# Projections as column tiles in two halves, a tail split by tile, and SyncE's general path in front: one change to a two-part attention kernel

## The chip, the cores and the metric

One core of a Trainium2 chip. The metric is the device time of one launch in microseconds (us): the median of a kernel's runs in the fast state. A granted TensorE clock, as a share of full speed, comes with each run. A profiled run also has a span, from its first to its last instruction, which is 1.7 to 1.9 us shorter than that run's own time.

## The reference

Two independent halves, joined along the last axis; inputs and outputs are bfloat16.

```python
def reference(A_x, A_wq, A_wk, A_wv, A_wo, B_x, B_wqkv, B_w_phi, B_wo):
    # A: softmax attention, S=2048, D=512, 32 query heads of 16, one key/value head
    q = (x @ wq).reshape(B, S, 32, 16).transpose(0, 2, 1, 3);  k = x @ wk;  v = x @ wv
    p = softmax(einsum("bhqd,bkd->bhqk", q, k) * 16 ** -0.5)
    a = einsum("bhqk,bkd->bhqd", p, v)...reshape(B, S, 512) @ wo
    # B: linear attention; features [softmax(u), softmax(-u)] of u = q @ w_phi and u = k @ w_phi
    kv = einsum("bhsf,bhsd->bhfd", phi_k, v);  z = phi_k summed over s
    o = einsum("bhqf,bhfd->bhqd", phi_q, kv) / (einsum("bhqf,bhf->bhq", phi_q, z) + 1e-6)
    b = o...reshape(B, S, 512) @ wo
    return concatenate([a, b], axis=-1)
```

## The kernel before

A small planner inside the kernel makes the program when it is built. Every piece of work is a job with an engine and an assumed duration; the planner simulates the engines, picks what to issue next, and writes one fixed, in-order program for each engine. The chip gets these orders as they stand. So a constant of the planner changes the order, and with it how many score blocks go which way.

Scores of part A are made in quads of four blocks. A quad goes one of two ways: ScalarE exponentiates it (two instructions `f_PT<-f_ps`, 128x1024), or VectorE turns it into bit patterns of powers (four `f_Z<-f_ps`) which GpSimd shifts (`f_Z<-f_Z`). Either way TensorE multiplies with the values in groups of four column tiles. All projections are done between these groups.

```python
    def job(self, name, eng, dur, fn, after=(), mode=None, nb=0, frees=(), rel=0.0, prio=5.0, ok=None):
        j = _Job(name, eng, dur, fn, after, mode, nb, frees, rel, prio, ok)
        ...
    # one of 92 projections: four full 128x128 matmuls in one go
    job(("pq", ch), "pe", 0.86, ..., mode="full", nb=1, ...)
    def proj_q(self, ch):
        ...
            for dc in range(4):
                mm = pe.matmul(ps[:, bank, :], lhsT=self.wq[:, dc, A * 128:A * 128 + 128],
                               rhs=xT[:, dc, qc * 512:(qc + 1) * 512], start=(dc == 0), stop=(dc == 3))
    # normalisation of a finished pair of heads: a VectorE product of two SBUF tensors
    job(("on", sc), "dve", 0.60, ...finish_sc3...)
    # jobs that the planner never lets run beside a GpSimd shift:
    LOCK = ("dS", "qw")
    # the planner's choice between a locked VectorE job and a shift that asked first
    if j.eng == "dve" and j.name[0] in self.LOCK:
        s, j = next((p for p in picks if p[1].eng == "pool" and p[1].asked <= s + self.NEAR ...), (s, j))
    # end of each engine's program: the fast path jumps over the general path
                e.br_eq(r, 0, there + "_over", there).branch_hint(ahead)
                with e.bass.body(there, valid_engines=[e.engine]):
                    ...general(name, e)...
    # tail: output tiles 2 and 3 copied and sent by ScalarE, 0 and 1 by VectorE and SyncE
        for i in (2, 0, 3, 1): ...
```

## Time and profile before

| | before |
|---|---|
| time, median of 3 runs | 713.73 us (712.76 to 714.05) |
| span of the profiled run | 711.0 us |
| double exponentials of part A on ScalarE | 700 |
| bit conversions on VectorE | 648 |
| first exponential starts | 9.25 us |
| last exponential ends | 695.18 us |

One budget is used all through, because ScalarE leads:

span = first exponential + floor + stalls + tail.

The floor is 0.904 us (the median from start to start) for each double exponential and 0.477 for each of the 64 exponentials of part B. The stalls are what is left up to the end of the last exponential. The tail is the rest. The stalls can also be summed from the trace, as everything above 0.905 us from start to start of neighbouring double exponentials; this sum is called the excess.

One more line: the normalisation. In this trace the three with no shift of GpSimd beside them took 681 to 691 ns and the slowest with one 1375, so the mean time hints at how much GpSimd slowed them.

```profile
L1879 DVE TENSOR_TENSOR f_On<-f_accS,f_denS 128x512 bf16<-128x512 f32 x16 | 15.3, 958 | 0.8 <-DMA f_denS<-f_denS 0.8
```

A line of the page has: line of the kernel, engine, operation, out<-in, shapes, count | busy us, mean ns of one | idle us of the engine just before, and what ended most of it.

### The profile page before, as it was taken

The page shows a single profiled execution, that of the slowest core. Times are in us where ns is not written, and L with a number is a line of the kernel's source. Part 1 is how long each engine was busy: PE and PEld are TensorE (multiplying, and loading weights), DVE is VectorE, ACT ScalarE, POOL GpSimd, SP SyncE. Part 2 cuts the span into 40 slices and gives each one's busy share as a digit, 9 for nine tenths or more (in the row PEclk, how much of TensorE's full clock was granted, in tenths as well). Part 3 has the DMA queues.
Part 4 walks back from the last instruction along what each step waited for, and adds up shares of the span by engine and source line. Part 5 has one row for each costly group of instructions (what it writes and reads, how often), then busy time and mean ns, then how long its engine had stood idle before and what let it go on. Part 6 is the DMA issues. An engine that isn't in the chain of part 4 may idle for free.

```text
span 711.0 us, 18172 instructions
## 1 busy us (share of the span) xinstructions
PE 669.8 (94%) x7493; PEld 211.0 (30%) x7548; DVE 620.6 (87%) x1039; ACT 683.7 (96%) x771; POOL 521.8 (73%) x522
## 2 busy tenths in 40 slices
PE   8999999999999999999999999999999999999995
PEld 3222223222323223332222322323332323333322
DVE  4789899998999999999788987889878989989974
ACT  5999999999999999999999999999999999999992
POOL 4488877777778667876878777678878787787870
PEclk9999999999999999999999999999999999999998
DMA  6611233110112110111110111111111210111212
GB/s 136 134 16 29 41 38 80 8 10 7 9 13 38 11 12 5 12 9 13 9 8 15 17 19 17 16 16 23 21 16 10 27 24 20 17 14 16 32 16 53
DMA packets 47890, 18.28 MB, mean 26 GB/s; under 512 B 38708, under 2 KB 45940, under 8 KB 47800
## 3 DMA queue, kind: packets, MB, share of 16 engines
q1 hardware_dynamic: 45400, 16.23, 18.0%
q8 instruction: 60, 0.98, 0.6%
q10 hardware_dynamic: 2400, 0.82, 0.5%
q14 instruction: 30, 0.25, 0.1%
HBM read 2.28 MB, written 4.19 MB: 9 GB/s over the span
## 4 chain that ended last, share of the span: by engine, by line
ACT 47%; PE 30%; DVE 20%; issue 1%; DMA 1%; POOL 1%; ACTq 0%; DVEq 0%
ACT f_PT L1647 45%; DVE f_Z L1752 11%; PE f_ps L1592 10%; PE f_ps L1812 8%; PE f_ps L1694 4%; PE f_ps L2246 2%; DVE f_ssum L2070 1%; DVE f_vS L2104 1%; ACT f_ET L2161 1%; PE f_ps L1582 1%; PE f_ps L1898 1%; DVE f_Wk L2216 1%; DMA f_AxT<-in_A_x_dram 1%; PE f_ps L2056 1%; DVE f_On L1879 1%
## 5 line engine op out<-in xcount | busy, mean ns | idle before, releaser
L1647 ACT ACTIVATE f_PT<-f_ps 128x1024 bf16<-128x1024 f32 x700 | 654.5, 1093 | 12.4 <-PE f_ps L1592 9.8
L1782 POOL INT64_ADD f_Z<-f_Z x486 | 512.7, 1055 | 167.5 <-DVE f_Z L1752 128.1
L1752 DVE TENSOR_SCALAR f_Z<-f_ps 128x512 int16<-128x512 f32 x648 | 426.0, 683 | 52.7 <-PE f_ps L1592 50.1
L1592 PE MATMUL f_ps<-f_QA,f_KR 32*128 32x512 bf16 x2048 | 280.2, 385 | 14.9 <-ACT f_PT L1647 11.3
L1812 PE MATMUL f_ps<-f_Z,f_VK 128*32 128x512 f16 x2592 | 227.5, 386 | 4.2 <-DVE f_Z L1752 1.6
L1592 PEld LDWEIGHTS f_ps<-f_QA,f_KR 32*128 32x128 bf16 x2048 | 70.4, 91 | 254.4 <-ACT f_PT L1647 224.8
L1694 PE MATMUL f_ps<-f_PT,f_VA 128*32 128x512 bf16 x1400 | 131.6, 385 | 0.1
L1812 PEld LDWEIGHTS f_ps<-f_Z,f_VK 128*32 128x32 bf16 x2592 | 56.4, 94 | 105.4 <-issue 61.2
L1694 PEld LDWEIGHTS f_ps<-f_PT,f_VA 128*32 128x32 bf16 x1400 | 33.6, 94 | 47.8 <-issue 44.7
L2216 DVE TENSOR_TENSOR f_Wk<-f_ps,f_wq 128x512 bf16<-128x512 f32 x32 | 21.9, 683 | 3.6 <-PE f_ps L2205 3.6
L1413 PE MATMUL f_ps<-f_ones,f_zero 128*128 128x512 bf16 (+4 forms) x112 | 20.2, 364 | 1.3 <-POOL f_zero L1432 1.3
L1419 DVE COPY f_accS<-f_ps 128x512 f32<-128x512 f32 x31 | 21.1, 680 | 0.0
L2104 DVE TENSOR_TENSOR f_vS<-f_ps,f_rs 128x1024 bf16<-128x1024 f32 x16 | 19.7, 1229 | 0.2 <-PE f_ps L2094 0.2
L2070 DVE TENSOR_REDUCE f_ssum<-f_Ek 128x64 f32<-128x1024 bf16 x16 | 19.3, 1205 | 0.0
L2161 ACT ACTIVATE f_ET<-f_ps 128x512 bf16<-128x512 f32 x32 | 18.8, 689 | 0.1
L2064 ACT ACTIVATE f_Ek<-f_ps 128x512 bf16<-128x512 f32 x32 | 18.2, 655 | 0.0
L1419 DVE CAST f_outB<-f_ps 128x512 bf16<-128x512 f32 x16 | 10.9, 683 | 6.7 <-PE f_ps L2246 6.7
L2154 PE MATMUL f_ps<-f_BxT,f_Wq 128*128 128x512 bf16 x56 | 14.8, 381 | 1.9 <-issue 1.0
L2246 PE MATMUL f_ps<-f_Bwo,f_oT 128*128 128x512 bf16 x57 | 15.0, 381 | 1.5 <-issue 1.0
L2094 PE MATMUL f_ps<-f_Bwv,f_BxT 128*128 128x512 bf16 x56 | 15.0, 381 | 1.2 <-DVE f_Z L1752 0.8
L1879 DVE TENSOR_TENSOR f_On<-f_accS,f_denS 128x512 bf16<-128x512 f32 x16 | 15.3, 958 | 0.8 <-DMA f_denS<-f_denS 0.8
L2056 PE MATMUL f_ps<-f_Wk,f_BxT 128*128 128x512 bf16 x53 | 14.1, 380 | 1.8 <-issue 1.5
(95 smaller groups left out, 281.7 us busy)
## 6 DMA issues: line engine op xcount, KB each, us to landing
f_denS<-f_denS SPq DMA_DIRECT2D x124, 30.0 KB, 3.1
out_dram<-f_outB SPq DMA_DIRECT2D x16, 128.0 KB, 1.8
f_denC<-f_accS SPq DMA_DIRECT2D x124, 2.0 KB, 1.7
f_denS<-f_denC SPq DMA_DIRECT2D x124, 2.0 KB, 1.7
out_dram<-f_outA SPq DMA_DIRECT2D x14, 128.0 KB, 2.8
f_On<-f_Ot SPq DMA_DIRECT2D x60, 16.0 KB, 1.8
f_Bwv<-in_B_wqkv_dram SPq DMA_DIRECT2D x1, 512.0 KB, 4.2
f_Bwo<-in_B_wo_dram SPq DMA_DIRECT2D x1, 512.0 KB, 4.5
```

The source lines that it names most:

```text
L1419: self.add("dve", lambda v: v.tensor_copy(out=out, in_=in_), reads=reads, writes=writes)
L1592: return pe.matmul(self.ps[:, bank, :], lhsT=self.KR[32 * g:32 * g + 32, sc % 2, kap * 128:(kap + 1) * 128], rhs=self.QA[32 * g:32 * g + 3 ...
L1647: self.add("act", lambda a: a.activation(out=PT[:, sl[0]:sl[0] + size, :], in_=ps[:, b0:b0 + size, :], func=ACT.Exp), reads=[("PS", b0 + i ...
L1694: mm = pe.matmul(ps[32 * g:32 * g + 32, bank, :], lhsT=VA[:, kap, :], rhs=PT[:, slots[g], :], start=start, stop=stop, tile_position=(0, 32 ...
L1752: self.add("dve", lambda v: v.tensor_scalar(out=o, in0=ps[:, bank, :], scalar1=self.Z1, scalar2=self.Z0, op0=ALU.mult, op1=ALU.add), reads ...
L1782: fn = lambda g: g.int64_add(out=b, in0=a, in1=256 * t * 0x1000100010001)
L1812: mm = pe.matmul(ps[32 * g:32 * g + 32, bank, :], lhsT=self.VK[:, t, kap, :], rhs=Zf[:, sl[g], :], start=start, stop=stop, tile_position=( ...
L2070: self.add("dve", lambda v: v.tensor_reduce(out=ssum[:, r, :], in_=Ek[:, r].rearrange("p a h f -> p (a h) f"), axis=AX.X, op=ALU.add), rea ...
L2104: self.add("dve", lambda v: v.tensor_tensor(out=vS[:, :, :, 0:16], in0=v3, in1=rs.unsqueeze(3).to_broadcast([128, 2, 32, 16]), op=ALU.mult ...
L2161: self.add("act", lambda e: e.activation(out=self.ET[:, sl, :], in_=self.ps[:, bank, :], func=ACT.Exp, scale=1.0 - 2.0 * a), reads=[("PS", ...
L2216: self.add("dve", lambda v: v.tensor_tensor(out=o, in0=i, in1=w.unsqueeze(3).to_broadcast([128, 2, 16, 16]), op=ALU.mult), reads=[("PS", b ...
L2246: mm = pe.matmul(ps[:, bank, :], lhsT=oT[:, r, C, :], rhs=self.Bwo[:, C, :], start=(C == 0), stop=(C == 3))
```

## The change

Its intent: a whole projection delays the next scores, so do it in the value products' own tiling mode and in two halves between them; shorten the tail; take a jump off the end; start a little earlier. A dozen constants of the planner were changed with it, and normalisations were locked. The core of the diff:

```diff
     def job(self, name, eng, dur, fn, after=(), mode=None, nb=0, ...):
+        if nb and name[0] in self.SPLIT and dur > 0.8:
+            first = (name[0] + "0",) + name[1:]
+            self.job(first, eng, dur / 2, self.of_part(fn, 0), after, mode, nb, (), rel, prio, ok)
+            return self.job(name, eng, dur / 2, self.of_part(fn, 1), [first], mode, 0, frees, 0.0, self.SECOND)
...
+    def terms(self):
+        return range(4) if self.part_no is None else range(2 * self.part_no, 2 * self.part_no + 2)
...
-            for dc in range(4):
-                mm = pe.matmul(ps[:, bank, :], lhsT=self.wq[:, dc, A * 128:A * 128 + 128], rhs=xT[...], start=(dc == 0), stop=(dc == 3))
+            for dc in terms:
+                for g in range(4):
+                    mm = pe.matmul(ps[32 * g:32 * g + 32, bank, a:a + n], lhsT=self.wq[:, dc, A * 128 + 32 * g:A * 128 + 32 * g + 32], rhs=xT[...], start=(dc == 0), stop=(dc == 3), tile_position=(0, 32 * g))
... (the same in five other projections)
-        for i in (2, 0, 3, 1):
-            o, eng = oa[:, i, :], "act" if i > 1 else "dve"
+        for i in range(4):
+            o = oa[:, i, :]
+            if i % 2 == 0:   # ScalarE copies tiles 0 and 2, VectorE adds up tiles 1 and 3
...
-    LOCK = ("dS", "qw")
+    LOCK = ("dS", "qw", "on", "kvfin")
-    PLEFT = 8.0   QS = 0.9   ZLOW = 4   LEFT = 8   AGE = 3.0   AGED = 0.8   DBUSY = 3.0   T_B = (54.0, 600.0)
+    PLEFT = 20.0  QS = 0.5   ZLOW = 3   LEFT = 16  AGE = 2.0   AGED = 0.6   DBUSY = 5.0   T_B = (43.0, 620.0)
+    SPLIT = ('bk', 'bv', 'bq', 'pq', 'op', 's8')   SECOND = 1.3   FIRST = dict(sp=2)
...
+                if first is not None:                  # SyncE only
+                    S.emit(name, e, sems, k, first)
+                    e.br(there + "_main")              # early jump over the general path
+                    slow()                             # the general path
+                    e.bass.switch_bb(there + "_main", outer)
...
+                    e.br_ne(r, 0, there, there + "_over")   # at the end: fall through
```

(Constants shown several to a line. Cut: the first 128 key columns and the first query chunk done in halves, some small part B reductions, the flag's place.)

## The prediction

> **What bounds the kernel now.** I read the page first: busy shares, the chain, then the costliest groups.
>
> ```profile
> PE 669.8 (94%) x7493; PEld 211.0 (30%) x7548; DVE 620.6 (87%) x1039; ACT 683.7 (96%) x771; POOL 521.8 (73%) x522
> ...
> ACT 47%; PE 30%; DVE 20%; issue 1%; DMA 1%; POOL 1%; ACTq 0%; DVEq 0%
> ...
> L1647 ACT ACTIVATE f_PT<-f_ps 128x1024 bf16<-128x1024 f32 x700 | 654.5, 1093 | 12.4 <-PE f_ps L1592 9.8
> L1752 DVE TENSOR_SCALAR f_Z<-f_ps 128x512 int16<-128x512 f32 x648 | 426.0, 683 | 52.7 <-PE f_ps L1592 50.1
> ```
>
> ScalarE is busy 96%, nearly all of it in 700 double exponentials, and leads the chain. Score blocks come in quads of four; a quad is exponentiated either by ScalarE (two instructions, 700/2 = 350 quads) or as bits by VectorE and GpSimd (four instructions, 648/4 = 162 quads). The planner inside the kernel decides which, so a change may move work between engines.
>
> Second, ScalarE's waits and the chain in order of time, because a busy ScalarE is not one at its best pace:
>
> ```profile
> ACT f_PT L1647 <- PE f_ps L1592: 9.8, 12, 6.1
> ACT f_ET L1946 <- DVE f_ET L1942: 5.9, 1, 5.9
> ```
> ```profile
> 9.27 66.34 ACT f_PT L1647 x72
> ...
> 524.88 33.01 ACT f_PT L1647 x36
> ...
> 694.40 0.98 PE f_ps L1812 x16
> ```
>
> Long runs show 33.01/36 = 0.917 us each. From start to start of neighbours in the trace (667 pairs) the median is 0.904, the mean 0.937; the sum above 0.905 is 22.2 us. The wait view hides this: neighbours overlap by about 0.17 us, so a late start shows as a smaller overlap, not as idle time. The ScalarE budget is: first exponential at 9.25; 700 x 0.904 + 64 exponentials of part B x 0.477 = 663.3; stalls 22.6; last exponential ends at 695.18; tail 15.8. Sum 711.0, the span.
>
> Third, what makes a start late: a stretch with a projection (L1582).
>
> ```profile
> 203.57 0.39 PE L1592 MATMUL f_ps<-f_QA,f_KR 32*128 32x512 bf16 x3
> ...
> 203.90 1.04 PE L1582 MATMUL f_ps<-f_AxT,f_wq 128*128 128x512 bf16 x4
> ...
> 204.87 0.39 PE L1592 MATMUL f_ps<-f_QA,f_KR 32*128 32x512 bf16 x3
> ```
>
> Scores follow scores 1.30 us later, where ScalarE wants them every 0.904. With two score buffers some lateness is absorbed, not all. Of the 22.2 us, 10.7 fall in windows with a projection or output product, though these are about a tenth of the windows.
>
> Fourth, the tail:
>
> ```profile
> 699.81 0.69 DVE L1419 CAST f_outB<-f_ps 128x512 bf16<-128x512 f32 x1 [1.20 <-PE f_ps L2246]
> ...
> 700.56 0.44 DVE L1942 STREAM_SHUFFLE f_ET<-f_ps 128x256 f32<-128x256 f32 x1
> ...
> 704.66 0.60 ACT L1956 ACTIVATE f_outA<-f_ps 128x512 bf16<-128x512 f32 x1 [0.47 <-ACT f_outA L1956]
> 705.29 1.12 ACTq L1961 DMA_DIRECT2D out_dram<-f_outA  x1
> ```
>
> Leftovers of part B (its last output products, copied at 699.81) hold VectorE, so the finish starts 5.4 us after the last exponential. The last output copy is ScalarE's second one; its transfer is seen landed at 707.86. SyncE's sequencer records then show the compare-and-branch ending at 708.24 and its next record only at 710.75: 2.51 us in which nothing but the jump over the general path happens.
>
> [...] group starts follow each other in 0.216 us in one mode and in 0.311 to 0.322 across modes (row to column 0.315, column to row 0.312, row to full 0.317), so about 0.10 per switch. [...] within a group of four value products starts are 3 ns apart, so four column tiles cost 0.216, as one full matmul does. [...]
>
> **The change part by part.**
>
> *Projections.* 92 of them (16 each of bk, bv, bq, pq, s8 and 12 op), each 4 full matmuls (0.864), become 16 matmuls on four column tiles: 4 x 0.216 = 0.864 again. Nothing is saved in streaming. But they are now in the value products' mode and, except the first, cut in two halves of 0.432 with other work between. A window with one value product is 0.315 + 0.312 = 0.627; with one half projection instead 0.843; both under 0.904. A whole full projection makes 0.317 + 0.648 + 0.311 = 1.276. I counted in the instruction order how much TensorE work stands between each score pair and the next, with these steps, leaving aside the windows that also hold part B exponentials (load above 1.35). Work above 0.904 sums to about 37 us before and 17 us after; windows between 1.1 and 1.35 fall from 85 to 13. Switches are no argument: 161 into full mode become 77, but into column mode 585 become 674.
>
> *What the planner moves.* Order lists: 710 double exponentials (+10), 628 bit conversions (-20), 471 GpSimd shifts (-15), 2512 column matmuls on bits (-80). Five quads went to ScalarE: +10 x 0.904 = +9.0 us on the bounding engine. TensorE loses 20 x 0.216 on bits and gains 5 x 0.216. VectorE loses about 20 x 0.6 = 12 us plus 12 small additions of 0.48; it is not the bound.
>
> *Stalls.* 22.6 x 17/37 = 10.4 us if they scale with excess work. Smaller excesses are better absorbed by the second buffer, so it may be 6; the stalls of value products alone (11 us before) may also stay, so it may be 15. I take 10: -12.6 us.
>
> *Head.* Before, keys (1.02) and two whole query projections (1.73) precede the first scores at 8.82. Now: 128 key columns (4 x 0.056), half of one query chunk, its other half, copied by ScalarE (about 0.4 for 256 columns), so the first exponential at about 8.45: -0.8 us.
>
> *Tail.* Part B's last product now stands 34 exponentials before the end, so it blocks nothing. But the two partial sums of output tiles stand after the last value product, behind seven fills[...], then two copies 0.68 on VectorE, so the shuffle starts about 4.0 us after the last exponential instead of 5.4: -1.4. From there on, tiles alternate between ScalarE and VectorE in both halves, so the last transfer starts near 704.5 on the old clock instead of 705.29, and lands about 0.6 earlier. SyncE falls through instead of jumping: -2.5. ScalarE still jumps, but its last issue now ends 2.3 us earlier, hidden. Tail 15.8 - 1.4 - 0.6 - 2.5 = 11.3. The jump that SyncE now takes after two input transposes lies beside a wait of the input chain and costs nothing visible.
>
> *Sum.* 8.45 + (710 x 0.904 + 64 x 0.477 = 672.4) + 10 + 11.3 = 702.1 of span, against 711.0. The median time exceeds the span by 2.7; I take 2, the profiled run's own difference (712.87 - 711.0): 704 us, -1.4%.
>
> **Rivals.** (a) The stalls stay and only the ten exponentials are added: 702.1 + 12.6 = 714.7 span, 717 us. For it: TensorE busy is already 94%, and half of the stalls are not at projections. Against: counted excess work more than halves. (b) The stalls nearly vanish (3 us): 697 us, faster by over 2%. For it: most windows now hold at most 0.843. Against: 74 windows hold 1.0 to 1.1, above 0.904. (c) The bank held between the halves starves the bit path: only four banks are left for it, sums and projections; VectorE already waits 50.1 us for scores. Fewer bits quads than 157 can't follow, as the order is fixed, but the score group would wait in TensorE's queue and ScalarE with it: 708 to 712. (d) The tail's last denominators: from the copy of the sums to the normalisation takes 15.1 us before (three chained transfers); 20 exponentials (18 us) now follow the copy, so it fits, with 3 us to spare; if not, +2.
>
> **Range and chances.** Stalls of 5 to 15 give 699 to 709; head and tail add 1 either way. Range 698.5 to 709.5. Two per cent faster is below 699.5, which needs stalls under about 5.5: 0.15. Slower by 2% is 728, outside every rival: 0.02.
>
> **What would show it.** First exponential near 8.45; 710 of them; the start-to-start median unchanged at 0.904, its mean down from 0.937 to about 0.92; excess in windows with projections down from 10.7 to some 3; shuffle 4 us after the last exponential; SyncE's branch followed by its drain within 0.2 us. The prediction is wrong if excess over 0.905 stays near 22, if half projections wait for each other's banks, or if the last normalisation waits for its transfer.

The sum is 8.45 + 672.4 + 10 + 11.3 = 702.1 us of span. In the tail the step for the thirteen matmuls before the shuffle is cut; its 4.0 us and the -1.4 stand as the estimates they were. With the trace's own numbers, 0.216 us from start to start and 0.38 for the last, those matmuls take 12 x 0.216 + 0.38 = 2.97. The -2.5 for the jump rests on the 2.51 us of the trace alone.

## The result

| | before | after |
|---|---|---|
| time, median of 4 runs | 713.57 (712.76 to 714.05) | 712.35 (711.68 to 712.62) |
| span of the profiled run | 711.0 | 709.9 |
| first exponential | 9.25 | 8.80 |
| double exponentials; floor | 700; 663.3 | 710; 672.4 |
| stalls | 22.6 | 16.1 |
| last exponential ends | 695.18 | 697.22 |
| tail | 15.8 | 12.7 |

The ratio is 0.9983, 95% interval 0.9965 to 1.0: the same. A ratio here is the mean time of one kernel's fast runs over that of the other's in the same rounds, so it is not quite the ratio of the medians. The prediction was 704 us with a range of 698.5 to 709.5, so it was wrong: the right direction, far too much. The budget says where. Against a predicted span of 702.1 the first exponential is 0.35 us later, the stalls are 6.1 larger and the tail is 1.4 longer: 7.8 together, the whole miss.

The page after:

```profile
PE 682.6 (96%) x8606; PEld 207.0 (29%) x8609; DVE 602.6 (85%) x1009; ACT 689.3 (97%) x782; POOL 498.4 (70%) x507
...
ACT 60%; PE 31%; DVE 4%; POOL 1%; DMA 1%; SPq 1%; issue 1%; POOLq 0%; DVEq 0%
...
L1701 ACT ACTIVATE f_PT<-f_ps 128x1024 bf16<-128x1024 f32 x710 | 661.9, 1124 | 4.3 <-PE f_ps L1748 2.3
L1806 DVE TENSOR_SCALAR f_Z<-f_ps 128x512 int16<-128x512 f32 x628 | 418.2, 684 | 74.3 <-PE f_ps L1646 69.9
...
L1933 DVE TENSOR_TENSOR f_On<-f_accS,f_denS 128x512 bf16<-128x512 f32 x16 | 11.2, 702 | 7.4 <-DMA f_denS<-f_denS 7.4
```

The chain now rests on ScalarE for 60% instead of 47%; ScalarE's idle time before the exponentials fell from 12.4 to 4.3 us; ten more exponentials are there, exactly as predicted. The normalisation takes 702 ns instead of 958, which is the lock at work. Of the 31 normalisations the 24 with no shift beside them take 677 to 692 ns; three take 990 to 1309, and each of these had a shift beside it for 449 to 765 ns. Not every overlap shows: the other four, with a shift beside them for 15 to 499 ns, take 680 to 684. So the lock holds in the plan, and mostly, not always, on the chip.

The waits of ScalarE and VectorE after (us in total, times, longest):

```profile
ACT f_ET L2003 <- DVE f_ET L1999: 6.0, 1, 6.0
ACT f_PT L1701 <- PE f_ps L1748: 2.3, 2, 2.2
ACT f_PT L1701 <- PE f_ps L1646: 1.5, 4, 0.7
DVE f_On L1933 <- DMA f_denS<-f_denS: 7.4, 1, 7.4
```

Two of the misses can be read here. First, a single wait of 2.2 us for a value product (L1748). The timeline shows it:

```profile
602.95 0.39 PE L1646 MATMUL f_ps<-f_QA,f_KR 32*128 32x512 bf16 x3
...
603.27 1.05 PE L1866 MATMUL f_ps<-f_Z,f_VK 128*32 128x512 f16 x16
...
604.15 0.60 PE L1748 MATMUL f_ps<-f_PT,f_VA 128*32 128x512 bf16 x8
...
604.59 1.02 ACT L1701 ACTIVATE f_PT<-f_ps 128x1024 bf16<-128x1024 f32 x1 [2.16 <-PE f_ps L1748]
```

The scores had long been there. ScalarE had no place to write to: the ring of exponentials was full, because the order puts one value product of bits after the other (L1866) in front of the value product that would empty it. This is no chance of one run: three later runs of the same order show the same stall, 2.07, 2.29 and 2.31 us over the usual 0.904 (here 2.31).

The halves have a part in the order that led there. Between 596.62 and 604.15 no value product of exponentials started: from 597.67 on, four windows in a row went to halves of output products (L1955), and then came the bits. That the halves are the cause is not shown: the later run with whole projections in this order has the stall too.

Second, the tail, in the timeline of VectorE, SyncE's queue and TensorE:

```profile
690.10 0.68 DVE L1933 TENSOR_TENSOR f_Ot<-f_accS,f_denS 128x512 bf16<-128x512 f32 x1
...
692.06 3.40 SPq L1909 DMA_DIRECT2D f_denS<-f_denS  x4
695.50 2.45 SPq L1939 DMA_DIRECT2D f_On<-f_Ot  x4
698.15 0.69 DVE L1933 TENSOR_TENSOR f_On<-f_accS,f_denS 128x512 bf16<-128x512 f32 x1 [7.37 <-DMA f_denS<-f_denS]
...
700.55 0.81 PE L1975 MATMUL f_ps<-f_wo_pad,f_On 128*128 128x512 bf16 x3 [0.56 <-DMA f_On<-f_Ot]
```

The last-but-one pair of heads is normalised at 690.10, 23.3 us after its sums were copied (before: 15.8). Its result must be moved by a transfer that SyncE issues, but SyncE's program has the denominators of the last pair in front, and those wait for a transfer of their own until 692.06. So the move is issued at 695.50, and the partial output sums (L1975), which need it, start at 700.55. Their copies end at 702.67 and the shuffle starts at 702.72, 5.5 us after the last exponential (697.22), not 4.0.

The jump is gone as foreseen: SyncE's compare-and-branch ends at 709.66 and its next record stands at 709.71. Before, it was 708.24 and 710.75.

### The profile page after: what moved, and what is told of

The parts are those of the page before. It is cut to its first block, busy times and chain, and to the rows that moved or that the text cites. A ratio compares the mean times of both kernels' runs of the same rounds, so it can differ in the third digit from the quotient of the medians.

```text
span 709.9 us, 20307 instructions
## 1 busy us (share of the span) xinstructions
PE 682.6 (96%) x8606; PEld 207.0 (29%) x8609; DVE 602.6 (85%) x1009; ACT 689.3 (97%) x782; POOL 498.4 (70%) x507
## 4 chain that ended last, share of the span: by engine, by line
ACT 60%; PE 31%; DVE 4%; POOL 1%; DMA 1%; SPq 1%; issue 1%; POOLq 0%; DVEq 0%
ACT f_PT L1701 57%; PE f_ps L1646 11%; PE f_ps L1866 8%; PE f_ps L1748 4%; DVE f_Z L1806 2%; ACT f_Ek L2127 2%; PE f_ps L1955 1%; PE f_ps L2319 1%; POOL f_Z L1836 1%; PE f_ps L2225 1%; ACT f_ET L2231 1%; PE f_ps L1443 1%; PE f_ps L2275 1%; PE f_ps L2300 1%; PE f_ps L1628 1%
## 5 line engine op out<-in xcount | busy, mean ns | idle before, releaser
L1701 ACT ACTIVATE f_PT<-f_ps 128x1024 bf16<-128x1024 f32 x710 | 661.9, 1124 | 4.3 <-PE f_ps L1748 2.3
L1836 POOL INT64_ADD f_Z<-f_Z x471 | 489.0, 1038 | 192.3 <-DVE f_Z L1806 153.3
L1806 DVE TENSOR_SCALAR f_Z<-f_ps 128x512 int16<-128x512 f32 x628 | 418.2, 684 | 74.3 <-PE f_ps L1646 69.9
L1866 PE MATMUL f_ps<-f_Z,f_VK 128*32 128x512 f16 x2512 | 216.8, 385 | 5.0 <-PE f_ps L1866 1.8
L1748 PE MATMUL f_ps<-f_PT,f_VA 128*32 128x512 bf16 x1420 | 133.0, 385 | 0.1
L1866 PEld LDWEIGHTS f_ps<-f_Z,f_VK 128*32 128x32 bf16 x2512 | 53.1, 94 | 95.2 <-issue 58.5
L1748 PEld LDWEIGHTS f_ps<-f_PT,f_VA 128*32 128x32 bf16 x1420 | 34.1, 94 | 50.6 <-issue 45.2
L1443 PE MATMUL f_ps<-f_ones,f_zero 128*128 128x512 bf16 (+6 forms) x109 | 21.7, 371 | 1.5 <-POOL f_zero L1462 1.3
L2162 PE MATMUL f_ps<-f_Bwv,f_BxT 128*32 128x512 bf16 x256 | 19.6, 383 | 0.3
L2225 PE MATMUL f_ps<-f_BxT,f_Wq 128*32 128x512 bf16 x256 | 19.6, 383 | 0.2
L1628 PE MATMUL f_ps<-f_AxT,f_wq 128*32 128x512 bf16 (+1 forms) x272 | 19.5, 371 | 0.3
L2319 PE MATMUL f_ps<-f_Bwo,f_oT 128*32 128x512 bf16 x256 | 19.6, 382 | 0.1
L2119 PE MATMUL f_ps<-f_Wk,f_BxT 128*32 128x512 bf16 x256 | 19.6, 383 | 0.0
```

The source lines that it names most:

```text
L1443: mm = pe.matmul(ps[m * i:m * i + m, bank, 0:n].rearrange("p (a n) -> p a n", n=128), lhsT=zero[0:r, 0:m], rhs=rhs, start=start, stop=star ...
L1628: mm = pe.matmul(ps[32 * g:32 * g + 32, bank, a:a + n], lhsT=self.wq[:, dc, A * 128 + 32 * g:A * 128 + 32 * g + 32], rhs=xT[:, dc, qc * 51 ...
L1701: self.add("act", lambda a: a.activation(out=PT[:, sl[0]:sl[0] + size, :], in_=ps[:, b0:b0 + size, :], func=ACT.Exp), reads=[("PS", b0 + i ...
L1748: mm = pe.matmul(ps[32 * g:32 * g + 32, bank, :], lhsT=VA[:, kap, :], rhs=PT[:, slots[g], :], start=start, stop=stop, tile_position=(0, 32 ...
L1806: self.add("dve", lambda v: v.tensor_scalar(out=o, in0=ps[:, bank, :], scalar1=self.Z1, scalar2=self.Z0, op0=ALU.mult, op1=ALU.add), reads ...
L1836: fn = lambda g: g.int64_add(out=b, in0=a, in1=256 * t * 0x1000100010001)
```

## The experiments

Letters for theories in the expectations belong to the runs of one batch only. "Stalls", "floor" and "tail" are those of the budget, read in each run's profile. First the whole table; the median of "before" lay between 712.7 and 713.9 in each batch, and batches ran on different chips, so a difference of about 1 us between runs of different batches says nothing.

| run | projections | normalisations | exponentials | first | stalls | tail | span | median | ratio, 95% |
|---|---|---|---|---|---|---|---|---|---|
| before | full, whole | free | 700 | 9.25 | 22.6 | 15.8 | 711.0 | 713.57 | 1 |
| after | tiles, halves | locked | 710 | 8.80 | 16.1 | 12.7 | 709.9 | 712.35 | 0.9983, 0.9965 to 1.0 |
| e1_on_free | tiles, halves | free | 700 | 8.74 | 29.8 | 14.0 | 715.9 | 717.66 | 1.0067, 1.0048 to 1.0086 |
| e2_whole | tiles, whole | free | 700 | 8.72 | 25.4 | 13.8 | 711.3 | 712.36 | 0.9989, 0.9973 to 1.0006 |
| e3_full | full, whole | free | 700 | 9.10 | 22.2 | 15.7 | 710.4 | 712.15 | 0.9999, 0.9971 to 1.0028 |
| e4_before_on | kernel before | locked | 706 | 9.82 | 24.9 | 39.6 | 743.1 | 743.47 | 1.0426, 1.0383 to 1.0469 |
| e5_same_whole | tiles, whole, order held | locked | 710 | 8.98 | 36.0 | 13.4 | 730.7 | 730.96 | 1.0231, 1.02 to 1.0261 |
| e6_same_full | full, halves, order held | locked | 710 | 8.72 | 20.0 | 12.7 | 713.8 | 715.56 | 1.0016, 0.9987 to 1.0046 |
| e7_jump_back | as after | locked | 710 | 9.04 | 16.0 | 16.2 | 713.6 | 715.10 | 1.0007, 0.9977 to 1.0037 |
| e8_on_told | tiles, halves | free, told | 704 | 8.72 | 23.2 | 10.7 | 709.6 | 710.70 | 0.9948, 0.9913 to 0.9982 |
| e9_near | tiles, halves | locked | 706 | 8.69 | 19.0 | 10.9 | 707.3 | 709.18 | 0.9948, 0.9925 to 0.9971 |
| e10_order | tiles, halves, own order | locked | 700 | 8.79 | 18.2 | 10.0 | 700.4 | 702.09 | 0.985, 0.9833 to 0.9866 |
| e16_order_halves2 | tiles, halves, own order | locked | 698 | 8.83 | 16.7 | 12.0 | 699.1 | 701.65 | 0.9831, 0.9814 to 0.9849 |
| e12_order_told | tiles, halves, own order | free, told | 700 | 8.71 | 18.0 | 10.2 | 700.3 | 702.88 | 0.986, 0.9841 to 0.9879 |
| e11_order_whole | tiles, whole, own order | locked | 698 | 8.69 | 16.5 | 8.5 | 695.2 | 697.28 | 0.98, 0.9766 to 0.9833 |
| e15_order_whole2 | tiles, whole, own order | locked | 698 | 9.28 | 16.8 | 9.3 | 696.9 | 698.47 | 0.9784, 0.9768 to 0.9801 |
| e13_order_full | full, whole, own order | locked | 696 | 9.04 | 22.1 | 9.6 | 700.5 | 703.86 | 0.9868, 0.9843 to 0.9893 |
| e17_order_full2 | full, whole, own order | locked | 698 | 9.03 | 21.4 | 8.9 | 700.9 | 700.96 | 0.9816, 0.9795 to 0.9837 |
| e18_whole_as_full | full, whole, e11's order | locked | 698 | 8.38 | 23.9 | 7.9 | 701.7 | 704.52 | 0.9881, 0.9842 to 0.9919 |
| e14_order_before | kernel before, own order | locked | 696 | 10.12 | 23.5 | 10.9 | 704.3 | 707.06 | 0.9909, 0.9882 to 0.9936 |

### Is it the lock that ate the gain?

The ten extra exponentials cost 9.0 us, and the lock on normalisations is the part that most obviously takes room from the bits. So the first theory was: without it the gain of the halves appears.

```diff
-    LOCK = ("dS", "qw", "on", "kvfin")
+    LOCK = ("dS", "qw", "kvfin")
```

> The changed kernel, except that the normalisation of part A ('on') is taken off the planner's list of VectorE work that must not run beside GpSimd. Theory A (this one rule ate the gain: it lets normalisations wait 24 to 53 us for a gap in GpSimd, which keeps the sums in their banks and turns bit quads into exponentials): 700 exponentials instead of 710, last normalisation about 15 us after its copy, stalls of ScalarE 10 to 14 us instead of 16, tail below 12 us, time 697 to 703 us. Rival B (TensorE is the true bound, quads merely move): time within 2 us of the changed kernel, 710 to 714, with the stalls grown to 25. Rival C (VectorE and GpSimd slow each other when the normalisation is free): normalisations of 0.9 us instead of 0.7 and the bit path late, time 704 to 709.

Measured: 717.66 us. The ten exponentials are gone (700), but stalls grew from 16.1 to 29.8. The theory falls: in this order, freeing the normalisations gained nothing. What went wrong is in two views, the page and the waits:

```profile
L1933 DVE TENSOR_TENSOR f_On<-f_accS,f_denS 128x512 bf16<-128x512 f32 x16 | 16.7, 1045 | 1.8 <-DMA f_denS<-f_denS 1.8
```
```profile
ACT f_PT L1701 <- PE f_ps L1646: 10.6, 19, 2.8
```

A normalisation takes 1045 ns instead of 702. The planner reckons with 0.60 us of engine time for one that takes 0.68 undisturbed, so the fixed order comes 0.35 us late with each of them. The longest wait has a second cost, and another cause. TensorE stood still for 1.95 us for a bit conversion, and in the table by stretches (busy us of each engine, then PEclk, the granted TensorE clock as a share of full speed) the clock then fell to half:

```profile
329.00:332.00 3.00, 2.76 (x34) 0.72 (x30) 3.00 (x7) 3.00 (x4) 2.75 (x3) 1.00 0.38 23
332.00:335.00 3.00, 1.05 (x7) 0.24 (x9) 2.93 (x7) 1.49 (x2) 0.61 (x1) 0.76 0.39 18
335.00:338.00 3.00, 3.00 (x26) 0.49 (x22) 1.72 (x4) 1.26 (x2) 1.98 (x2) 0.50 0.00 0
338.00:341.00 3.00, 3.00 (x32) 0.58 (x28) 2.08 (x4) 3.00 (x5) 1.13 (x2) 0.61 0.00 0
```

In the 50 us from 300 to 350, the excess is 6.2 us, against 0.9 in the changed kernel. The clock fell 1.4 us after the gap of 1.95 us without a recorded matmul began, and stayed at 0.50 for 6.8 us. The clock is not the whole loss: the one run at 0.997 has a span of 714.6, against 710.5 for the changed kernel.

No normalisation made TensorE wait here. From 328.41 to 333.43 VectorE did `kvfin`, ten small instructions that close part B's sums. The planner reckons 2.7 us for it and keeps it locked in both kernels. On the chip it took 2.17 us in the changed kernel, with no shift beside it, and 5.02 us here, with shifts beside it for 3.83 us. Its eight products, in the changed kernel and then here:

```profile
L2207 DVE TENSOR_TENSOR f_KVn<-f_kvS,f_mask 128x128 bf16<-128x128 f32 x8 | 1.7, 281 | 0.0
L2207 DVE TENSOR_TENSOR f_KVn<-f_kvS,f_mask 128x128 bf16<-128x128 f32 x8 | 4.5, 635 | 0.0
```

So about 5 of the 13.7 us that the stalls grew by are an accident of this order, and this run does not tell what the freed normalisations cost.

### Halves and column tiles, with normalisations free

The next two undo, on top of the run just told, the halves alone, and then the column tiles too; the planner is free to make a new order each time. A fourth run in the batch put the lock into the kernel before.

```diff
-    SPLIT = ('bk', 'bv', 'bq', 'pq', 'op', 's8')
+    SPLIT = ()
```

> As e1_on_free, and the projections not cut in two: four column tiles in one piece. Theory A with halves as the means against stalls: stalls of ScalarE 5 to 8 us above e1_on_free's, mostly in windows with projections, time 3 to 8 us above it. Rival (the halves are worth nothing, the mode alone counts): within 1.5 us of e1_on_free.

> As e1_on_free, and the projections whole and as full matmuls, as in the kernel before, everything else (tail, head, SyncE, planner constants) as changed. If the gain of the projections is real and only hidden in the changed kernel, this is 4 to 9 us above e1_on_free and 4 to 8 us below the kernel before (head and tail alone). If column tiles are worth nothing it equals e1_on_free within 1.5 us.

Measured: 712.36 and 712.15 us, stalls 25.4 and 22.2. Both are better than halves in this setting, and neither differs from before. All three orders hold 700 exponentials, so they differ mainly in stalls (full matmuls also have a tail longer by 1.7 to 1.9 us). That was the first sign that what a form of projection is worth depends on the order around it.

```diff
-    LOCK = ("dS", "qw")
+    LOCK = ("dS", "qw", "on")
```
(in the kernel before, with the flag's place moved to the end of three programs)

> The kernel before, and the normalisation put on the planner's list of VectorE work that must not run beside GpSimd; the flag of the fast path falls to the very end in this plan and its waits are moved there, so the tail is longer and the last exponential is what to compare. Theory A: 706 exponentials instead of 700, normalisations 20 to 50 us after their copy, last exponential ending 3 to 8 us later than the 695.2 of before. Rival (the rule costs nothing): last exponential at 695 to 696.

Measured: 743.47 us, ratio 1.0426, 1.0383 to 1.0469. This run is inconclusive. Its order left part B over for the end: part B's last exponentials stand after part A's, and the finish then waited 22.2 us in one piece. Up to the last exponential of part A (703.54 us, 706 of them) its stalls were 24.9.

### The same order, one thing taken away

To see what halves and tiles do by themselves, the order must be held. The next two keep the changed kernel's order of jobs, its 710 exponentials and its lock, and change only what TensorE executes. In the first, the first half's place holds the whole projection, and the second's only two columns of the last term.

```diff
-        return range(4) if self.part_no is None else range(2 * self.part_no, 2 * self.part_no + 2)
+        return [(d, 0, 512) for d in range(4)] if self.part_no is None else \
+            [(0, 0, 512), (1, 0, 512), (2, 0, 512), (3, 0, 510)] if self.part_no == 0 else [(3, 510, 512)]
```

> The changed kernel with its exact order of jobs and its 710 double exponentials and 628 bit conversions, but each projection done whole (still in column tiles) where its first half stood; where the second half stood only the last two columns of the last term are left, so that nothing else moves. Theory A (the prediction's: a start is late because the window holds more than 0.904 us of TensorE work, so halves are what removes stalls): each whole projection makes a window of 0.315 + 3 x 0.216 + 0.312 = 1.28 us at least, excess over 0.905 grows from 15.8 by 4 to 8 us, median 716 to 720 us. Theory B (the stalls that count come from TensorE waiting for bits and sums; projections are absorbed by the two score buffers and the ring of exponentials whether whole or halved): excess within 2 us of 15.8, median 711 to 714 us.

Measured: 730.96 us, 18.6 over the changed kernel, stalls 36.0. ScalarE now waits for scores 53 times where the changed kernel has 4:

```profile
ACT f_PT L1701 <- PE f_ps L1646: 14.3, 53, 1.2
```

Theory A was right in direction and the effect was more than twice what it gave. In this order halves are worth 18.6 us.

```diff
-                for g in range(4):
-                    mm = pe.matmul(ps[32 * g:32 * g + 32, bank, :], lhsT=...32 * g:...32 * g + 32..., tile_position=(0, 32 * g))
+                mm = pe.matmul(ps[:, bank, :], lhsT=...the 128 columns..., ...)
```
(in all six projections, halves kept)

> The changed kernel with its exact order, halves kept, but each half as two full 128x128 matmuls instead of eight column tiles, so only the tiling mode of the projections differs. Theory A (window load): a half beside value products now costs two switches more, about 0.2 us; in windows with value products and a half that is 0.843 + 0.2 = 1.04, so excess grows by 3 to 6 us, median 715 to 718 us. Theory B (absorbed): within 2 us, 711 to 714 us.

Measured: 715.56 us, 3.2 over the changed kernel, stalls 20.0 instead of 16.1, the lower end of theory A. Column tiles beside value products are worth about 3 us here.

### SyncE's jump, put back

```diff
-    FIRST = dict(sp=2)
+    FIRST = {}
```

> The changed kernel with SyncE's general path back behind the branch, so that SyncE jumps at the end as before; nothing else differs. If laying it out in front is worth what the prediction says: SyncE's compare-and-branch again stands 2.4 to 2.6 us before its next record, and span and median grow by 2.3 to 2.5 us, to 714.7 us. Rival: ScalarE's own jump, whose next record was at 709.66 where SyncE's was at 709.71, already hid part of it, or the early jump cost something at the start that now comes back: growth under 1.5 us, and the first exponential moves by over 0.1 us.

Measured: 715.10 us, 2.75 over the changed kernel; span +3.7. The last exponential ends only 0.15 later, so nearly all of it is tail. SyncE's compare-and-branch ends at 710.74 and its next record starts at 713.29: 2.55 us, 2.5 more than in the changed kernel, as predicted. ScalarE jumps in both kernels, and its time was hidden only just: in the changed kernel its next record stands at 709.58, SyncE's at 709.71. What SyncE does in the 2.5 us is not shown; the run shows that they come and go with this layout. The other 1.0 came before the branch, in the last transfers: SyncE's third issue took 1.83 us here and 1.07 there. At the start the jump that SyncE now does not take gains nothing: the first exponential is 0.24 later, not earlier.

### The order told the true duration

If the unlocked run failed because its order was built on 600 ns, an order built on 350 ns more should do better.

```diff
 (on top of the first experiment)
-            job(("on", sc), "dve", 0.60, ...
+            job(("on", sc), "dve", 0.95, ...
```

> The changed kernel with normalisations free to run beside GpSimd (as the first experiment, which lost 5 us), but with the order built on the 0.95 us that they take there instead of 0.60: 704 double exponentials, 640 bit conversions. Theory C (the first experiment stalled because the fixed order was built on too short a normalisation, so that bits and sums came late and TensorE stood still): excess falls from 27.9 to 18 us or less, ScalarE's wait for scores from 10.6 to under 5 us, and the median to 707 to 711 us, under the changed kernel. Theory D (GpSimd slowed normalisations are not the cause; stalls fill whatever the lighter ScalarE leaves): excess stays above 22, median 713 to 718 us.

Measured: 710.70 us, 7 us better than unlocked and untold, 1.7 better than the changed kernel. Between the two theories the result is mixed: the time is in C's range, but stalls (23.2; excess 22.5) are at D's bound. Normalisations still take long:

```profile
L1933 DVE TENSOR_TENSOR f_On<-f_accS,f_denS 128x512 bf16<-128x512 f32 x16 | 16.5, 1030 | 7.8 <-DMA f_denS<-f_denS 7.8
```

ScalarE's wait for scores fell from 10.6 to 3.1 us, but its waits for value products, the full ring, rose from 1.9 to 5.5. This does not show that the wrong duration was a cause: in this order no shift fell beside `kvfin` (2.17 us), and from 300 to 350 us the excess is 1.0 instead of 6.2. That is 5.2 of the 6.6 us by which the stalls fell.

### Orders made for the form

So far every order but the changed kernel's own had been inherited. The next runs give each form its own: the planner's constants were drawn some thousand times for each form, and the order that by the planner's own reckoning ends first was run. The reckoning only picks; the chip decides. The first run changes one constant: how soon a GpSimd shift that asked first must be able to start, in us, for the planner to let it go before a locked VectorE job.

```diff
-    NEAR = 0.15
+    NEAR = 0.1
```

> The changed kernel with one constant of its planner other[...]. Locked normalisations stay. 706 double exponentials and 636 bit conversions instead of 710 and 628, and no order of jobs is kept. Theory E (the ten exponentials are a price of this one order, not of the halves, the column tiles or the lock): stalls stay at 14 to 17 us, exponentials give back 4 x 0.904 = 3.6, the tail no longer waits for the denominators (12.7 to about 11), median 706 to 709 us. Theory D (whatever a lighter ScalarE leaves, stalls fill): excess grows to 19 or more, median 711 to 714 us.

Measured: 709.18 us, 3.2 better than the changed kernel. Four exponentials fewer give 3.6, the tail 1.8, and 2.9 come back as stalls (16.1 to 19.0). It lies between the theories, just outside E's time and D's stalls.

```diff
-    NEAR = 0.15   AGE = 2.0   AGED = 0.6   T_B = (43.0, 620.0)   SECOND = 1.3
+    NEAR = 0.1    AGE = 2.5   AGED = 0.8   T_B = (43.0, 590.0)   SECOND = 0.8
```

> The changed kernel with five constants of its planner other (NEAR 0.1, AGE 2.5, AGED 0.8, T_B (43, 590), SECOND 0.8), the lock kept: 700 double exponentials and 648 bit conversions, as many as before the change. Theory E: first exponential 8.8 + floor 663.3 + stalls 14 to 18 + tail 11 = 697 to 701 of span, median 699 to 703 us: the changed projections then show the gain that the prediction saw in them. Theory D: excess 24 or more, median 709 to 713 us.

Measured: 702.09 us. Theory E holds, with stalls 0.2 above its range: 700 exponentials with stalls of 18.2 and a tail of 10.0. With the lock kept, the ten extra exponentials were a price of one order, not of halves, tiles or lock.

```diff
-    SPLIT = ('bk', 'bv', 'bq', 'pq', 'op', 's8')   NEAR = 0.15  AGE = 2.0  AGED = 0.6  T_B = (43.0, 620.0)  LEFT = 16  ZLOW = 3  QS = 0.5
+    SPLIT = ()                                     NEAR = 0.1   AGE = 1.5  AGED = 0.8  T_B = (35.0, 590.0)  LEFT = 8   ZLOW = 4  QS = 0.9
```

> The changed kernel with whole column-tile projections (no halves) and planner constants searched in the same way for that form (NEAR 0.1, AGE 1.5, AGED 0.8, T_B (35, 590), LEFT 8, ZLOW 4, QS 0.9), the lock kept: 698 double exponentials, 652 bit conversions. It tells what halves are worth when each form has an order of its own. Theory A (halves remove window load): stalls stay 6 to 10 us above those of the run with halves in its own order, so with 2 exponentials fewer the median is 4 to 8 us above it. Theory D: within 2 us of it.

Measured: 697.28 us, and here my expectation fell on both counts. Whole projections in an order of their own stall no more than halves in theirs (16.5 against 18.2), and the kernel is 4.8 us faster. The lines of its page and waits:

```profile
L1701 ACT ACTIVATE f_PT<-f_ps 128x1024 bf16<-128x1024 f32 x698 | 651.8, 1093 | 2.3 <-PE f_ps L1646 1.1
L1806 DVE TENSOR_SCALAR f_Z<-f_ps 128x512 int16<-128x512 f32 x652 | 428.0, 683 | 51.1 <-PE f_ps L1646 48.6
```
```profile
ACT f_PT L1701 <- PE f_ps L1646: 1.1, 2, 0.7
```

against the run with halves in an order of its own:

```profile
L1701 ACT ACTIVATE f_PT<-f_ps 128x1024 bf16<-128x1024 f32 x700 | 653.2, 1115 | 5.5 <-PE f_ps L1646 3.5
```
```profile
ACT f_PT L1701 <- PE f_ps L1646: 3.5, 7, 1.2
ACT f_PT L1701 <- PE f_ps L1748: 1.0, 1, 1.0
```

```diff
 (on top of the run told 0.95)
-    AGE = 2.0   AGED = 0.6   T_B = (43.0, 620.0)   SECOND = 1.3
+    AGE = 1.5   AGED = 0.8   T_B = (50.0, 610.0)   SECOND = 0.8
```

> Normalisations free beside GpSimd, the order built on 0.95 us for them (as the eighth experiment), with AGE 1.5, AGED 0.8, T_B (50, 610), SECOND 0.8: 700 double exponentials, 648 bit conversions. If freeing them was bad only because the order was built on a wrong duration, this is as good as the locked run with 700 exponentials, within 2 us. If normalisations beside GpSimd themselves bring stalls that no constant in the order foresees, excess is 4 us or more above that of the locked run, and so is the median.

Measured: 702.88 us, stalls 18.0, within 1 us of the locked run: with the duration told, free and locked are alike, in one order of each. That the duration is the reason is not shown.

### Are these differences the form's, or two orders' luck?

A second order for whole and for halves, one for full matmuls, and one for the kernel before.

```diff
 e15:  SPLIT = ()   NEAR = 0.1   AGE = 3.0  AGED = 0.8  T_B = (50.0, 620.0)  ZLOW = 2  DBUSY = 4.0
 e16:               NEAR = 0.1   AGE = 1.5  AGED = 0.8  T_B = (35.0, 600.0)  ZLOW = 2  DBUSY = 4.0  QS = 0.3  PLEFT = 8.0  SECOND = 0.8
 e13:  full, whole; NEAR = 0.05  AGE = 2.0  AGED = 0.6  T_B = (35.0, 620.0)  ZLOW = 2  DBUSY = 3.0  QS = 0.7  PLEFT = 8.0  LEFT = 8
 e14:  kernel before, LOCK = ("dS", "qw", "on", "kvfin"); NEAR = 0.05  AGE = 1.5  T_B = (35.0, 590.0)  QS = 0.7
```

> The changed kernel (lock, head, tail, SyncE's layout) with whole projections as full 128x128 matmuls and planner constants searched for that form (NEAR 0.05, AGE 2, AGED 0.6, T_B (35, 620), LEFT 8, ZLOW 2, QS 0.7, PLEFT 8, DBUSY 3): 696 double exponentials, 656 bit conversions. If column tiles are worth the switches that they save: 2 to 4 us slower than the whole column-tile order (697.3), so 699 to 702 us. If they are worth nothing once the order is made for the form: 695 to 698 us.

> The kernel before, nothing of the change but the lock on normalisations, with planner constants searched in the same way (NEAR 0.05, AGE 1.5, AGED 0.8, T_B (35, 590), LEFT 8, ZLOW 4, QS 0.7, PLEFT 8, DBUSY 3): 696 double exponentials, 656 bit conversions. If the gains of the runs with searched constants are order and lock, not projections: first exponential 9.25 + floor 659.7 + stalls 17 to 19 + tail 13 (jump and old finish) = 699 to 701 of span, 701 to 703 us. If the projections' form carries it: stalls of 22 or more and 706 us or more. The flag of the general path may stand late and lengthen the tail; if so I take last exponential's end instead, 686 to 688 against 690 or more.

> A second order for whole column-tile projections, from other constants (NEAR 0.1, AGE 3, AGED 0.8, T_B (50, 620), LEFT 16, ZLOW 2, QS 0.5, PLEFT 20, DBUSY 4): also 698 and 652. It tells how far two orders of one form lie apart. If the order's luck is small, within 2 us of 697.3; if it is as large as the difference of forms seen (5 us), 700 to 704 us.

> A second order for halves (NEAR 0.1, AGE 1.5, AGED 0.8, T_B (35, 600), SECOND 0.8, QS 0.3, ZLOW 2, LEFT 16, PLEFT 8, DBUSY 4): 698 double exponentials, 652 bit conversions, as in the whole-projection order. If halves lose to whole ones by their own mechanism (more column and row switches, banks held longer): stalls of 18 or more, 700 to 703 us. If the 702.1 was one unlucky order and its two more exponentials: 695 to 699 us.

Measured: 703.86, 707.06, 698.47 and 701.65 us. Two orders of one form lie 1.2 us apart for whole and 0.4 for halves, so the 4 us between these forms are more than the luck of one order. The halves' second order has the time that I gave for "halves lose by their own mechanism", but not its stalls: it has as many exponentials as the whole ones and stalls of 16.7, and loses in the tail (12.0 against 8.5 and 9.3). Its sister e10 loses by two exponentials (1.8), stalls (1.7) and tail (1.5). Of e10's excess, 2.5 us lie around a stretch of half clock at 324.9, after a `kvfin` of 5.04 us; the two whole orders have no such stretch. So neither order of halves stalls more by itself than the whole ones.

The kernel before, with nothing but the lock and constants, gains 6.9 us on its batch. Its stalls of 23.5 and its time meet the second of my two readings, that the projections' form carries the rest. But the run is not clean: `kvfin` met shifts and took 5.30 us, TensorE stood still for 2.48 us at 314.8 and ran at half clock after it. 3.7 us of the excess lie there, and 1.5 around a second stretch of half clock at 529.5; without them the stalls would be about 18, as in the first reading. The four runs had clocks of 0.985 to 0.995. So this run does not decide between the two.

Full matmuls looked 5 us worse than whole tiles, more than I had given either way, with one order to show for it, and with lower clocks in those runs (0.992 to 0.997, against 0.999 and 1.0 in e15). Two more runs: a second order for full matmuls, and the order of e11 held with full matmuls.

```diff
 e17:  full, whole; NEAR = 0.05  AGE = 3.0  AGED = 0.6  T_B = (35.0, 590.0)  LEFT = 8  DBUSY = 3.0
 e18:  e11's constants and order; each group of four column tiles is one full matmul
```

> A second order made for whole full matmuls (NEAR 0.05, AGE 3, AGED 0.6, T_B (35, 590), LEFT 8, ZLOW 3, QS 0.5, PLEFT 20, DBUSY 3): 698 double exponentials, 652 bit conversions. If column tiles carry the gain: stalls of 20 to 23 us again and a median of 701 to 705. If the first full order was unlucky: stalls of 16 to 18 and 697 to 699.

> The best kernel so far (whole column-tile projections in their own order, 697.3 us) with the order held and each group of four column tiles as one full matmul. If switches into and out of the full mode are what costs: stalls up by 3 to 7 us from 16.5, median 700 to 704. If the mode is worth nothing for whole projections: within 1.5 us of 697.3.

Measured: 700.96 and 704.52 us. Stalls of 21.4 and 23.9 seem to settle it, but the second number must not be read alone. Its clock was 0.98 to 0.99 in all four runs, and the view by stretches of the profiled one shows where:

```profile
8.00:14.00 6.00, 5.49 (x63) 2.45 (x63) 5.79 (x16) 5.62 (x7) 3.25 (x14) 1.00 0.55 117
14.00:18.00 4.00, 2.12 (x16) 0.62 (x16) 1.03 (x5) 2.78 (x4) 0.00 (x0) 1.00 0.31 68
18.00:22.00 4.00, 3.88 (x36) 1.16 (x36) 2.75 (x8) 3.07 (x3) 0.00 (x0) 0.53 0.64 131
22.00:26.00 4.00, 3.67 (x18) 0.90 (x18) 0.00 (x0) 2.98 (x3) 0.00 (x0) 0.50 0.60 131
26.00:30.00 4.00, 4.00 (x33) 1.04 (x31) 2.98 (x9) 2.56 (x4) 0.00 (x0) 0.50 0.62 131
30.00:34.00 4.00, 4.00 (x23) 0.76 (x19) 1.45 (x3) 3.06 (x4) 0.00 (x0) 0.50 0.77 143
```

TensorE had no recorded matmul for 1.76 us at 15.4 and then ran at half clock for 17 us, while inputs were still loading. It waited for a transfer of the input A_x, which released it at 17.15; in e11 the same wait was 0.44 us long, at 16.15. So the gap is not the matmuls' own. Excess over 0.905 in the first 50 us is 7.9 there and 1.4 in e11; after 50 us it is 15.4 against 14.2. So with the order held, column tiles were worth 1.2 us in stalls, and the rest of the profiled run's stalls was the gap and the clock in the head; the other three runs were not profiled.

The two own orders of full matmuls lie 2.9 us apart, more than those of the other forms. In them 2.9 us (e13) and 3.7 us (e17) of the excess lie around a stretch of half clock that follows `kvfin`, which took 4.69 us in both (3.70 and 3.85 in the whole-tile orders). What is left of their stalls, about 19 and 18, is 1 to 3 us more than that of whole tiles.

For the forms with orders of their own, runs of like clock can be compared. Mean span of the runs whose granted clock was 0.997 or more (how many): whole tiles 695.4 (3) and 696.8 (4); full 700.5 (1) and 699.1 (3); halves 700.1 (2) and 699.8 (4); the changed kernel 710.5 (4); the kernel before 710.9 (17). The kernel before in its own order has no such run; its best is 703.6 at 0.995, where e13 has 700.9.

## Why the prediction was wrong, point by point

**What bounds the kernel: right.** ScalarE leads, its median step stayed 0.904 us in every run, and the excess agrees with the budget's stalls within 2 us.

**The cost of column tiles: right.** They are no shorter than full matmuls (383 ns each against 379 to 381, groups 0.215 to 0.226 apart); they save switches of mode, about 0.10 us each (0.311 to 0.322 from start to start across modes instead of 0.216 within one). With the order held this gave 3.2 us beside halves and 1.2 beside whole ones.

**Ten more exponentials, +9.0: right to the count**, with 628 conversions and 471 shifts.

**Stalls of 10: wrong. This is the step that failed**, "22.6 x 17/37 = 10.4 us if they scale with excess work". Stalls by the kind of window between two exponentials:

| excess over 0.905, us | windows with a projection | other part B work | value products only | sum |
|---|---|---|---|---|
| before | 11.1 | 3.7 | 7.5 | 22.2 |
| scaled by 17/37 | 5.1 | 1.7 | 3.4 | 10.2 |
| after | 5.4 | 1.8 | 8.6 | 15.8 |

The ratio was right for the windows that the change touches, to 0.3 us, and by the numbers also for part B's other work. It was applied to value-product windows too, which hold nothing of what the change altered. They did not shrink with it: 7.5 us in 437 windows before, and after, without the one full-ring stall of 2.3, 6.3 us in 363 windows, 17 ns per window both times. The full-ring stall came on top. So of the 5.6 us by which the sum was missed, 2.9 are these windows and 2.3 the full ring. The prediction named this alternative ("the stalls of value products alone (11 us before) may also stay, so it may be 15") and then chose 10. With 15 it would have said 709. Its 11 us held part B's other work too; value products alone were 7.5. Its "about a tenth of the windows" is low as well: 130 of 667 here.

The runs with the order held bear out which windows respond. With whole projections (e5) windows with a projection stall 27.5 us instead of 5.4, with full matmuls (e6) 10.3; value-product windows, without the full-ring stall, 4.4 and 4.5 instead of 6.3. So they do not grow with the projections, but their rate is no constant (12 ns there, 9 to 25 ns in own orders), and that before and after agree at 17 is in part luck.

**Tail of 11.3: off by 1.4.** Jump -2.5 was right (2.55 when put back), and the transfers' 0.6 fits what is left. (One reading was off: 707.86 is when SyncE saw its own second transfer landed; ScalarE's last one landed at 708.14, just before the branch.) The shuffle's -1.4 did not come: 5.5 us after the last exponential, 5.4 before. Part B's leftovers are out of the way, as foreseen; what took their place is a late normalisation, near the prediction's rival (d) but one pair earlier. The prediction gave the last pair 15.1 us from copy to normalisation; it took 19.8, and the pair before it, whose transfer queued behind, 23.3. In e11, with 16.5 and 18.5 us for these two pairs, the shuffle starts 0.8 us after the last exponential.

**Head -0.8: -0.45.** The first scores start at 8.37 instead of 8.82; I had expected 0.35 more. One profiled run each cannot settle this: kernels with the same head and column tiles start between 8.69 and 9.28.

**The rivals.** (a) stalls untouched, (b) nearly gone: neither. (c), banks held between the halves, was not isolated. For it: in own orders, windows with value products alone stall 8.5 and 5.3 us with halves, 3.5 and 4.0 with whole projections, while windows with projections stall 5.0 and 6.3 against 9.6 and 9.1. So in these orders halves have fewer stalls in one kind of window and more in the other, and the sum stays at 15.5 to 17.6; 2.5 of the 8.5 belong to e10's stretch of half clock. That the bank held in between is the reason is argued, not shown.

**Where the gain was.** The lesson of the runs goes beyond the failed step. Of halves, 18.6 us could be measured with the order held, yet an order made for whole projections stalls no more without them. An order is built around its forms: taking one away inside it measures how much the order leans on it, not what it is worth. The change as a whole stood still because its own order paid 9 us in exponentials for 6.5 us of stalls and 0.5 us of head, and the tail's 3.1 made the difference: 711.0 + 9.0 - 6.5 - 0.5 - 3.1 = 709.9. With other constants the same code runs at 701.7 to 702.1, and without the halves at 697.3 and 698.5, which beats both kernels: 0.98 and 0.9784 of before.

**Open.** Why halves lose in orders of their own (mostly in exponentials and tail, so perhaps by the orders alone; two orders of a form are few); whether better orders exist for any form (each had some thousand draws); how much of the gain of new orders the kernel before would have too. Three of the seven kernels with whole full matmuls had a clock below 0.993 on average over their runs, none of the four with whole tiles. In the profiled runs this looks like accidents of order: in e14, and in e13 and e17 as well, half clock follows a wait of TensorE at a `kvfin` that met shifts, in e18 a late transfer. When the clock halves is not explained. Waits without a recorded matmul of 0.81 (e17), 1.46 (e13), 1.76 (e18), 1.95 (e1) and 2.48 us (e14) were followed by a clock of 0.50, 1.4 to 3.2 us after they began, which lasted 3.4 to 17 us. One of 0.88 us at 486.81 in before was not, and the stretch at 166.3 us in e1 has less than 0.6 us of idle TensorE in all in the 12 us before it. After the last matmul of the program the clock fell 1.2 us later in before and 3.3 us later in the changed kernel.

## What to carry to other kernels

Scale a stall only over the windows that the change touches, and as a first estimate leave the others as they are. In a kernel with a planned order, compare forms each in an order made for it, at least two per form, and look at the granted clock before reading a difference of under one per cent (e11 ran in 697.3 us at 1.0 and in 701.6 at 0.992). A planner's rule that two things never run side by side is a rule of the plan: look in the trace whether it held. Here `kvfin`, reckoned at 2.5 or 2.7 us, took 2.17 to 5.30. When a changed kernel stands still, close a budget (first, floor, stalls, tail) before looking for a cause: here it showed at once that one term had been paid with another.
